# Building the Fourier stage's operands in token parts of 128, behind each transposed attention block

## Chip, cores and metric

One NeuronCore of a Trainium2 chip runs the whole program. The metric is the device time of one execution in microseconds (us), as the median of several runs. The engines of a core have queues of their own, each worked in order: TensorE (PE, with its weight loads as PEld), VectorE (DVE), ScalarE (ACT), GpSimd (POOL), and SyncE (SP) for most DMA.

## What is computed

Three blocks in a row, all in float32: windowed attention (4 batches, 8 heads, 576 tokens, head size 64, window 64), a mixer with a two-dimensional Fourier transform and a hidden layer, and a gated layer. The Fourier part is what the change touches.

```python
X = np.fft.fft(x, axis=1)          # 576 tokens
X = np.fft.fft(X, axis=2)          # 512 channels
mixed = np.real(X).astype(np.float32)
u = x + mixed
un = (u - mu) / np.sqrt(var + 1e-06)
ch = np.maximum(un @ w_ch1, 0.0) @ w_ch2
return (u + ch).astype(np.float32)
```

## The kernel before

**Layout.** The mixer's input and output live in one SBUF tile `uT` of 128 partitions x 4 channel groups x 2304 tokens (channels on partitions, transposed). The channels are permuted so that groups 0 and 1 hold channels 0 to 255 and groups 2 and 3 their mirror images; the real Fourier transform then needs only sums and differences of the two halves.

**Attention** (`attention`, L303 to L408) walks 36 blocks of 64 queries, nine for each batch b. A step computes scores (PE L314), masks and scales them (DVE L317), takes a maximum (DVE L320), exponentials (ACT L322), and one step later transposes (PE L329, copied out by ACT L331 as `pts`) and multiplies with the values (PE L342). `norm` divides (DVE L357, L358, L361). For each full pair of blocks `xt` (L365) transposes the result into one PSUM tile `xt`, of which there is one buffer, and ACT copies it into `uT` (L373). There are five such pieces i for a batch: four of 128 tokens and one of 64. When the last one is issued, `self.xdone = b` (L375).

**Fourier stage** (`dft`, L439 to L522), one call for each batch. L448 and L449 form the sum E and the difference O of the two channel halves over all 576 tokens (1152 elements a partition); L452 and L464 fold tokens t and 576-t onto each other (576 elements). All four run on DVE (`FP` is empty). Each result is split into a rounded high part (ACT, `eh` L457 and `oh` L465) and a remainder (POOL, `el` L458 and `ol` L466). One channel, the middle row, is handled apart: `gr` (POOL L460, L461) from O's first partition, its high part (ACT L462) and remainder (POOL L463) in two rows of `grow`. First-stage products on PE are groups of seven (with `grow`, L482, first and `mm3`, L124 to L126, behind it) or six matmuls; each group is copied out by ACT into `cp` (L491), split by ACT (L492) and POOL (L493). `cp` lies in columns of the E or O tile that are no longer needed: three places for each. The second stage (L496 to L521) makes the spectra and adds them to `uT`.

**Order.** `drive` (L1060 ff.) issues attention and, beside it, two lanes: decoding of weights (L155 to L165) and `dft(0)`, `ln(0)`, `dft(1)`. `dft(2)` and `dft(3)` are issued behind attention with high priority, in the lane `rest`. The tile framework then orders each engine's queue by priority and by a simulated time line, so that instructions can come earlier than they were issued. Behind attention follow the hidden layer (`h`, `acc`, L124 to L126, with `rl` from DVE L670) and the gated layer.

Of the kernel before, what the change touches and what calls it, by code (L numbers as in the profile page):

```python
# [9 lines left out]
F32 = mybir.dt.float32  # L10
F32R = mybir.dt.float32r
I32 = mybir.dt.int32
AF = mybir.ActivationFunctionType
ALU = mybir.AluOpType
# [3 lines left out]
B, H, S, D = 4, 8, 576, 64  # L18
# [23 lines left out]
FP = ()  # L42
# [65 lines left out]
class Kernel:  # L108
# [194 lines left out]
    def attention(self):  # L303
        nc, p, ps = self.nc, self.ap_, self.aps_
# [60 lines left out]
        def xt(n):  # L365
            b, j = divmod(n, NB)
            m, x = 64 if j == NB - 1 else 128, st.pop(("x", n))
            i = j // 2
            t = ps.tile([128, 4, 128], F32, tag="pt", bufs=2, name="xt") if XPT else ps.tile([128, 4, 128], F32, tag="xt", name="xt")
            for c in range(4):  # L370
                nc.tensor.transpose(t[:, c, 0:m], x[:m, 128 * c:128 * c + 128], self.ident[:m, :m])
            t0 = S * b + 128 * i
            nc.scalar.activation(out=self.uT[:, :, t0:t0 + m], in_=t[:, :, 0:m], func=AF.Copy)  # L373
            if j == NB - 1:
                self.xdone = b  # L375

# [34 lines left out]
    def open_dft(self):  # L411
        nc = self.nc
        self.dp, self.dft_es = self.pool("dft", side="left")
        p = self.dp
        self.xdone = -1
        w = [516, 516, 512, 512, 258, 870, 870, 870, 870]
        names = ["cdh", "cdl", "sdh", "sdl", "gt", "csh", "csl", "ssh", "ssl"]
        o = 0
        self.tab = p.tile([128, sum(w)], F32R, name="tab")
        for n, m in zip(names, w):  # L420
            setattr(self, n, self.tab[:, o:o + m])
            o += m
        self.cdh, self.cdl, self.sdh, self.sdl = (t.rearrange("p (k n) -> p k n", k=2) for t in (self.cdh, self.cdl, self.sdh, self.sdl))
        self.csh, self.csl, self.ssh, self.ssl = (t.rearrange("p (k n) -> p k n", k=3) for t in (self.csh, self.csl, self.ssh, self.ssl))
        self.grow = p.tile([128, 290], F32R, name="grow")
        nc.gpsimd.memset(self.grow[:].bitcast(F32), 0.0)
        self.tails = [[p.tile([128, 258], F32R, name=f"tail{i}{x}") for x in "ab"] for i in range(1)]
        for t in self.tails:
            for u in t:
                nc.gpsimd.memset(u[:].bitcast(F32), 0.0)  # L430

    def load_tables(self, i, after):
# [3 lines left out]
        self.nc.gpsimd.tensor_copy(self.tab[:, c.start:c.start + 4], after[:, 0:4])  # L436
        self.tc.keep_in_program_order(self.nc.gpsimd.dma_start(self.tab[:, c], self.aps["tab"][:, c]))

    def dft(self, b):  # L439
        nc, p = self.nc, self.dp  # L440
        x = self.uT[:, :, S * b:S * b + S]
        V, G, A = nc.vector, nc.gpsimd, nc.scalar
        EF = G if b in FP else V
        row = p.tile([1, S], F32, tag="row", name="row")
        nc.sync.dma_start(row, x[0:1, 2])
        E = p.tile([128, 2, S], F32, tag="E", name="E")
        O = p.tile([128, 2, S], F32, tag="O", name="O")
        EF.tensor_tensor(out=E, in0=x[:, 0:2], in1=x[:, 2:4], op=ALU.add)  # L448
        EF.tensor_tensor(out=O, in0=x[:, 0:2], in1=x[:, 2:4], op=ALU.subtract)  # L449
        fold = lambda t: t[:, :, 1:289]  # L450
        rev = lambda t: t[:, :, 575:287:-1]
        EF.tensor_tensor(out=fold(E), in0=fold(E), in1=rev(E), op=ALU.add)  # L452
        eh = p.tile([128, 2, 290], F32R, tag="eh", name="eh")
        el = p.tile([128, 2, 290], F32R, tag="el", name="el")
        oh = p.tile([128, 2, 290], F32R, tag="oh", name="oh")
        ol = p.tile([128, 2, 290], F32R, tag="ol", name="ol")
        A.activation(out=eh[:, :, 0:289], in_=E[:, :, 0:289], func=AF.Copy)  # L457
        G.tensor_tensor(out=el[:, :, 0:289], in0=E[:, :, 0:289], in1=eh[:, :, 0:289], op=ALU.subtract)  # L458
        gr = p.tile([1, 290], F32, tag="gr", name="gr")
        G.tensor_copy(gr[:, 0:1], O[0:1, 0, 0:1])  # L460
        G.tensor_tensor(out=gr[:, 1:289], in0=O[0:1, 0, 1:289], in1=O[0:1, 0, 575:287:-1], op=ALU.add)  # L461
        A.activation(out=self.grow[0:1, 0:289], in_=gr[:, 0:289], func=AF.Copy)  # L462
        G.tensor_tensor(out=self.grow[32:33, 0:289], in0=gr[:, 0:289], in1=self.grow[0:1, 0:289], op=ALU.subtract)  # L463
        EF.tensor_tensor(out=fold(O), in0=fold(O), in1=rev(O), op=ALU.subtract)  # L464
        A.activation(out=oh[:, :, 0:289], in_=O[:, :, 0:289], func=AF.Copy)  # L465
        G.tensor_tensor(out=ol[:, :, 0:289], in0=O[:, :, 0:289], in1=oh[:, :, 0:289], op=ALU.subtract)  # L466
        yield 5000
        ah = p.tile([128, 2, 258], F32R, tag="ah", name="ah")
        al = p.tile([128, 2, 258], F32R, tag="al", name="al")
        bh = p.tile([128, 2, 258], F32R, tag="bh", name="bh")  # L470
        bl = p.tile([128, 2, 258], F32R, tag="bl", name="bl")
        at, bt = self.tails[0]
        ts = [(0, 128), (128, 256), (256, 289)]
        for which in range(2):
            for i, (t0, t1) in enumerate(ts):
                m = t1 - t0
                ps = self.gtile()
                n = 256 if which else 258
                if which:
                    self.mm3(ps[:m, 0:n], [(oh[:, c, t0:t1], ol[:, c, t0:t1], self.sdh[:, c], self.sdl[:, c]) for c in range(2)])  # L480
                else:
                    nc.tensor.matmul(ps[:m, 0:n], lhsT=self.grow[:, t0:t1], rhs=self.gt, start=True, stop=False)  # L482
                    self.mm3(ps[:m, 0:n], [(eh[:, c, t0:t1], el[:, c, t0:t1], self.cdh[:, c], self.cdl[:, c]) for c in range(2)], first=False)
                if i < 2:
                    hi, lo = (bh, bl) if which else (ah, al)
                    hi, lo = hi[:, i, 0:n], lo[:, i, 0:n]
                else:
                    t = bt if which else at
                    hi, lo = t[0:33, 0:n], t[64:97, 0:n]
                cp = (O if which else E)[:m, i // 2, 288 * (i % 2):288 * (i % 2) + n]  # L490
                A.activation(out=cp, in_=ps[:m, 0:n], func=AF.Copy)  # L491
                A.activation(out=hi, in_=cp, func=AF.Copy)  # L492
                G.tensor_tensor(out=lo, in0=cp, in1=hi, op=ALU.subtract)  # L493
                yield 1700

        def stage2(out, lo_, hi_, tail, ch, cl, sl):  # L496
            self.mm3(out, [(hi_[:, k, sl], lo_[:, k, sl], ch[:, k], cl[:, k]) for k in range(2)], last=False)
            nc.tensor.matmul(out, lhsT=tail[:, sl], rhs=ch[:, 2], start=False, stop=False)
            nc.tensor.matmul(out, lhsT=tail[:, sl], rhs=cl[:, 2], start=False, stop=True)

        for c in range(2):
            sl = slice(128 * c, 128 * c + 128)
            pa = self.gtile()
            stage2(pa[:, 0:290], al, ah, at, self.csh, self.csl, sl)
            yield 2000
            pb = self.gtile()
            stage2(pb[:, 0:290], bl, bh, bt, self.ssh, self.ssl, sl)
            bs = p.tile([128, 290], F32, tag="bs", name="bs")
            A.activation(out=bs[:, 0:289], in_=pb[:, 0:289], func=AF.Copy)
            mi = p.tile([128, 290], F32, tag="mi", name="mi")  # L510
            pl = p.tile([128, 290], F32, tag="pl", name="pl")
            V.tensor_tensor(out=mi[:, 0:289], in0=pa[:, 0:289], in1=bs[:, 0:289], op=ALU.subtract)
            V.tensor_tensor(out=pl[:, 0:289], in0=pa[:, 0:289], in1=bs[:, 0:289], op=ALU.add)
            for k, u, w in ((c, mi, pl), (c + 2, pl, mi)):
                V.tensor_tensor(out=x[:, k, 0:289], in0=x[:, k, 0:289], in1=u[:, 0:289], op=ALU.add)
                G.tensor_tensor(out=x[:, k, 289:576], in0=x[:, k, 289:576], in1=w[:, 287:0:-1], op=ALU.add)
            yield 2000
        pa = self.gtile()
        stage2(pa[0:2, 0:290], al, ah, at, self.csh, self.csl, slice(256, 258))
        V.tensor_tensor(out=x[0:1, 2, 0:289], in0=pa[0:1, 0:289], in1=row[:, 0:289], op=ALU.add)  # L520
        V.tensor_tensor(out=x[0:1, 2, 289:576], in0=pa[0:1, 287:0:-1], in1=row[:, 289:576], op=ALU.add)  # L521
        yield 2000  # L522
# [820 lines left out]
```

## Time and profile before

| | |
|---|---|
| median of 3 runs (lowest, highest) | 779.79 us (777.94, 780.92) |
| the profiled execution's own time | 780.66 us |
| its span in the profile | 778.9 us |
| PE, DVE, ACT, POOL busy in the span | 755.9, 491.1, 340.5, 219.2 us |
| mean granted clock of TensorE | 0.991 of full |
| attention and what runs beside it | from 0 to about 150 us |

The profile is one execution, recorded by the hardware profiler. A table by stretches shows how long each engine was busy in each stretch and which share of full speed TensorE's clock was granted. A table of waits says for each idle time of an engine what it waited for. The time line lists instructions with start and duration, and in brackets the idle time ahead of an instruction and what ended it. The listing by source line gives the shortest, the median and the longest duration of one instruction.

### The profile page before, as it was taken

How to read it: one execution, taken by the hardware profiler on the slowest of the kernel's cores; microseconds unless marked ns; L12 is line 12 of the kernel's file. 1: busy time of each engine (PE TensorE's matmuls, PEld its weight loads, DVE VectorE, ACT ScalarE, POOL GpSimd, SP SyncE). 2: the span in 40 equal slices, each digit the busy share in tenths (PEclk: the TensorE clock that was granted, in tenths of full speed). 3: DMA queues.
4: the chain of work that ended last, by engine and by line, in shares of the span. 5: the costliest groups of instructions: out<-in, count | busy, mean ns of one | idle time of the engine just before them, and what ended most of it. 6: DMA issues, size and time to landing. Idle time of an engine off the chain costs nothing.

```text
span 778.9 us, 13646 instructions
## 1 busy us (share of the span) xinstructions
PE 755.9 (97%) x5018; PEld 727.3 (93%) x5018; DVE 491.1 (63%) x1126; ACT 340.5 (44%) x807; POOL 219.2 (28%) x268
## 2 busy tenths in 40 slices
PE   8879899999999999999999999999999999999998
PEld 7779688889999999999999999999999898989898
DVE  5677959594346489794588767644700468574662
ACT  5678797764233666341235323322742343130310
POOL 2135535534203551053712111121591021010100
PEclk9989999999999999999999999999999999999999
DMA  9996672353005878567746943953410020204023
GB/s 275 341 257 182 202 213 69 107 164 122 1 1 157 290 237 322 194 243 262 256 180 232 341 171 104 363 230 109 133 56 1 0 70 12 72 21 142 7 75 121
DMA packets 84770, 123.35 MB, mean 158 GB/s; under 512 B 24416, under 2 KB 61664, under 8 KB 84704
## 3 DMA queue, kind: packets, MB, share of 16 engines
q1 hardware_dynamic: 82912, 119.13, 46.0%
q0 software_dynamic: 576, 2.97, 1.2%
q8 instruction: 39, 0.64, 0.3%
q10 hardware_dynamic: 1216, 0.39, 0.2%
q14 instruction: 27, 0.22, 0.1%
HBM read 91.79 MB, written 30.67 MB: 157 GB/s over the span
## 4 chain that ended last, share of the span: by engine, by line
PE 82%; DVE 7%; DMA 6%; issue 2%; ACT 1%; POOL 0%; SPq 0%; DVEq 0%; ACTq 0%; POOLq 0%
PE w L124 7%; PE w L126 7%; PE w L125 7%; PE g L124 6%; PE c L124 6%; PE c L125 6%; PE c L126 6%; PE g L126 6%; PE g L125 6%; PE pv L342 3%; PE sc L314 3%; PE acc L126 2%; PE acc L125 2%; PE h L124 2%; PE acc L124 2%; PE h L126 2%
## 5 line engine op out<-in xcount | busy, mean ns | idle before, releaser
L164 ACT ACTIVATE set<-dec_w 128x256 fp32r<-128x256 f32 x103 | 41.7, 413 | 62.5 <-PE w L125 27.3
L798 POOL TENSOR_TENSOR u<-u 128x384 f32<-128x384 f32 x15 | 17.7, 1178 | 157.7 <-ACT u L797 139.0
L572 POOL TENSOR_TENSOR rq<-rq,mhalf 128x1 f32<-128x1 f32 (+1 forms) x24 | 15.7, 656 | 163.8 <-DVE rq L571 161.4
L322 ACT ACTIVATE s<-s,mx 128x128 f32<-128x128 f32 x144 | 46.2, 391 | 15.5 <-DVE mx L320 15.4
L158 ACT ACTIVATE dec_g<-dec_s 128x256 f32<-128x256 f32 x88 | 37.5, 429 | 32.9 <-DMA dec_s<-in_wi 16.7
L126 PE MATMUL acc<-rh,set 128*128 128x384 f32 x144 | 48.7, 338 | 0.0
L125 PE MATMUL acc<-rl,set 128*128 128x384 f32 x144 | 48.4, 336 | 0.0
L124 PE MATMUL acc<-rh,set 128*128 128x384 f32 x144 | 47.6, 337 | 0.5 <-DVE uT L655 0.5
L1004 DVE BATCH_NORM_STATS2 st<-u 128x6 f32<-128x512 f32 x18 | 12.4, 692 | 48.6 <-ACT u L1000 48.6
L160 DVE SCALAR_TENSOR_TENSOR dec_w<-dec_g,dec_w 128x256 int32<-128x256 int32 x88 | 41.3, 475 | 2.7 <-ACT dec_g L158 2.2
L314 PE MATMUL sc<-k,q 128*128 128x128 f32 x288 | 40.5, 290 | 2.5 <-DMA k<-in_k 1.4
L798 DVE TENSOR_TENSOR u<-w,u 128x384 f32<-128x384 f32 x44 | 24.3, 552 | 29.4 <-POOL u L798 24.3
L165 DVE TENSOR_TENSOR set<-dec_w,set 128x256 fp32r<-128x256 f32 x83 | 36.8, 451 | 8.2 <-PE h L125 3.8
L314 PEld LDWEIGHTS sc<-k,q 128*128 128x128 f32 x288 | 37.1, 203 | 4.0 <-DVE s L317 1.8
L317 DVE SCALAR_TENSOR_TENSOR s<-sc,mask 128x512 f32<-128x512 f32 x36 | 24.6, 686 | 25.4 <-PE pt L329 14.5
L159 DVE TENSOR_SCALAR dec_w<-dec_s 128x256 int32<-128x256 int32 x88 | 32.3, 377 | 6.4 <-DMA dec_s<-in_wi 3.9
L845 DVE TENSOR_TENSOR uT<-g,uT 128x384 f32<-128x384 f32 x36 | 19.3, 554 | 24.8 <-PE g L126 24.6
L670 DVE SCALAR_TENSOR_TENSOR rl<-h,rh 128x384 fp32r<-128x384 f32 x36 | 19.7, 548 | 20.1 <-ACT rh L669 20.1
L342 PEld LDWEIGHTS pv<-v,pts 128*64 128x64 f32 x576 | 24.7, 147 | 8.0 <-issue 4.5
L342 PE MATMUL pv<-v,pts 128*64 128x65 f32 x576 | 30.0, 237 | 1.6 <-DMA v<-in_v 1.6
L797 ACT ACTIVATE u<-w 128x384 f32<-128x384 f32 x29 | 14.1, 485 | 36.4 <-PE w L126 35.1
L655 DVE TENSOR_TENSOR uT<-acc,uT 128x384 f32<-128x384 f32 x48 | 25.2, 549 | 5.9 <-PE acc L126 5.7
(357 smaller groups left out, 2639.9 us busy)
## 6 DMA issues: line engine op xcount, KB each, us to landing
dec_s<-in_w SPq DMA_DIRECT2D x64, 256.0 KB, 3.3
v<-in_v SPq DMA_DIRECT2D x16, 520.0 KB, 5.4
xht<-xb SPq DMA_DIRECT2D x10, 768.0 KB, 10.0
xhm<-xb SPq DMA_DIRECT2D x10, 768.0 KB, 8.2
xlm<-xb SPq DMA_DIRECT2D x8, 768.0 KB, 9.2
k<-in_k SPq DMA_DIRECT2D x11, 512.0 KB, 5.7
xf<-u SPq DMA_DIRECT2D x18, 256.0 KB, 3.2
p<-xf SPq DMA_DIRECT2D x24, 192.0 KB, 3.6
```

The source lines that it names most:

```text
L124: mm(out, lhsT=lh, rhs=rh, start=first and i == 0, stop=False)
L125: mm(out, lhsT=lh, rhs=rl, start=False, stop=False)
L126: mm(out, lhsT=ll, rhs=rh, start=False, stop=last and i == n - 1)
L158: nc.scalar.activation(out=g, in_=s[:, :, 1].bitcast(F32), func=AF.Prelu, scale=2.0 ** -112, alpha=-2.0 ** 32)
L159: nc.vector.tensor_scalar(out=w, in0=s[:, :, 0], scalar1=29, scalar2=None, op0=ALU.logical_shift_right)
L160: nc.vector.scalar_tensor_tensor(out=w, in0=g[:].bitcast(I32), scalar=3, in1=w, op0=ALU.logical_shift_left, op1=ALU.bitwise_or)
L164: self.nc.scalar.activation(out=hi, in_=f, func=AF.Copy)
L165: (self.nc.gpsimd if self.bp is None else self.nc.vector).tensor_tensor(out=lo, in0=f, in1=hi, op=ALU.subtract)
L314: nc.tensor.matmul(sc[:, hp], lhsT=q[:, hp].rearrange("p a b -> p (a b)"), rhs=k[:, hp, o:o + 128], start=True, stop=True)
L322: nc.scalar.activation(out=s[:, hp], in_=s[:, hp], func=AF.Exp, bias=mx[:, hp:hp + 1])
L342: nc.tensor.matmul(o[r:r + 64, i // 4, 65 * (i % 4):65 * (i % 4) + 65], lhsT=pts[:, i // 2, 64 * (i % 2):64 * (i % 2) + 64], rhs=v[:, 65 * ...
L798: add = lambda eng, o, i, j: eng.tensor_tensor(out=o, in0=i, in1=j, op=ALU.add)
```

## The change

For batches 0 to 2, sums, differences and folds are no longer made in `dft` but piece by piece behind each `uT` copy of attention (`self.folds(b, i, t)`). `fold` adds and subtracts the piece: the lower channel half is read from the PSUM tile `t`, the upper half from `uT`. From piece 2 on, the tokens of that piece are mirrors of earlier ones, and the folds over those columns follow: 96, 128 and 64 columns. The folded difference goes into a tile F of its own, so that O stays whole. `gr` is folded in the same parts. Where the first stage of the batch before has been issued by then, the split into high and low parts is made in two parts as well (columns 65 to 288 behind piece 3, columns 0 to 64 behind piece 4); otherwise it is made whole in `dft`. Batch 3 makes all of it in `dft`, as one part, from `uT`. The product with `grow` moves from the first to the last place of its group. `cp` becomes a tile of its own with two buffers.

```diff
@@ xt
             nc.scalar.activation(out=self.uT[:, :, t0:t0 + m], in_=t[:, :, 0:m], func=AF.Copy)
+            self.folds(b, i, t)
@@ new functions
+    def fold(self, b, x, t, t0, m):
+        V, G = self.nc.vector, self.nc.gpsimd
+        if t0 == 0:
+            self.eo[b] = [self.dp.tile([128, 2, S], F32, tag=n, name=n) for n in ("E", "O", "F")]
+            self.gr[b] = self.dp.tile([1, 290], F32, tag="gr", name="gr")
+        E, O, F = self.eo[b]
+        gr = self.gr[b]
+        c = slice(t0, t0 + m)
+        V.tensor_tensor(out=E[:, :, c], in0=t, in1=x, op=ALU.add)
+        V.tensor_tensor(out=O[:, :, c], in0=t, in1=x, op=ALU.subtract)
+        a, z = max(1, S + 1 - t0 - m), min(289, S + 1 - t0)
+        if a < z:
+            r = slice(S - a, S - z, -1)
+            V.tensor_tensor(out=E[:, :, a:z], in0=E[:, :, a:z], in1=E[:, :, r], op=ALU.add)
+            V.tensor_tensor(out=F[:, :, a:z], in0=O[:, :, a:z], in1=O[:, :, r], op=ALU.subtract)
+            G.tensor_tensor(out=gr[:, a:z], in0=O[0:1, 0, a:z], in1=O[0:1, 0, r], op=ALU.add)
+        if t0 + m == S:
+            V.tensor_copy(F[:, :, 0:1], O[:, :, 0:1])
+            G.tensor_copy(gr[:, 0:1], O[0:1, 0, 0:1])
+
+    def fold_split(self, b, a, z):
...
+        A.activation(out=eh, in_=E[:, :, a:z], func=AF.Copy)
+        G.tensor_tensor(out=el, in0=E[:, :, a:z], in1=eh, op=ALU.subtract)
+        A.activation(out=oh, in_=F[:, :, a:z], func=AF.Copy)
+        G.tensor_tensor(out=ol, in0=F[:, :, a:z], in1=oh, op=ALU.subtract)
+        if a == 0:
...
+
+    def folds(self, b, i, t):
+        if b == B - 1:
+            return
+        t0, m = 128 * i, 64 if i == 4 else 128
+        self.fold(b, self.uT[:, 2:4, S * b + t0:S * b + t0 + m], t[:, 0:2, 0:m], t0, m)
+        if i == 3 and self.dft_read == b - 1:
+            self.fold_split(b, 65, 289)
+        elif i == 4 and b in self.fp:
+            self.fold_split(b, 0, 65)
@@ dft
-        EF.tensor_tensor(out=E, in0=x[:, 0:2], in1=x[:, 2:4], op=ALU.add)
-        EF.tensor_tensor(out=O, in0=x[:, 0:2], in1=x[:, 2:4], op=ALU.subtract)
...
+        if b == B - 1:
+            self.fold(b, x[:, 2:4], x[:, 0:2], 0, S)
+        if b not in self.fp:
+            self.fold_split(b, 0, 289)
+        eh, el, oh, ol = self.fp[b]
...
-                    nc.tensor.matmul(ps[:m, 0:n], lhsT=self.grow[:, t0:t1], rhs=self.gt, start=True, stop=False)
-                    self.mm3(ps[:m, 0:n], [...], first=False)
+                    self.mm3(ps[:m, 0:n], [...], last=False)
+                    nc.tensor.matmul(ps[:m, 0:n], lhsT=self.grow[:, t0:t1], rhs=self.gt, start=False, stop=True)
...
-                cp = (O if which else E)[:m, i // 2, 288 * (i % 2):288 * (i % 2) + n]
+                cp = p.tile([128, 258], F32, tag="cp", bufs=2, name="cp")[:m, 0:n]
...
+        self.dft_read = b
```

## Rows read from the trace of the kernel before

**Rows 1.** Page, span in 40 equal slices: PE busy tenths, granted clock in tenths.
```profile
PE   8879899999999999999999999999999999999998
PEclk9989999999999999999999999999999999999999
```

**Rows 2.** Stretches of 10 us: busy of PE, PEld, DVE, ACT, POOL; clock, DMA, GB/s.
```profile
40.00:50.00 10.00, 6.22 (x76) 5.55 (x74) 9.31 (x17) 7.81 (x24) 2.80 (x5) 0.95 1.10 289
50.00:60.00 10.00, 9.54 (x79) 8.94 (x79) 5.22 (x12) 6.61 (x21) 4.67 (x7) 0.71 0.76 218
...
80.00:90.00 10.00, 8.26 (x88) 6.99 (x86) 10.00 (x19) 7.50 (x18) 5.78 (x7) 1.00 0.73 216
90.00:100.00 10.00, 8.06 (x64) 6.08 (x64) 8.31 (x23) 7.37 (x22) 4.85 (x7) 0.83 0.49 133
...
110.00:120.00 10.00, 10.00 (x91) 9.33 (x90) 6.23 (x10) 8.49 (x26) 5.14 (x8) 1.00 0.82 289
...
130.00:140.00 10.00, 8.73 (x95) 6.94 (x92) 7.50 (x21) 7.84 (x20) 2.64 (x5) 1.00 0.11 29
...
150.00:160.00 10.00, 8.60 (x55) 8.21 (x53) 9.84 (x13) 5.67 (x16) 6.96 (x7) 1.00 0.82 255
160.00:170.00 10.00, 9.31 (x56) 9.00 (x55) 10.00 (x27) 6.80 (x20) 2.98 (x3) 1.00 0.37 112
```

**Rows 3.** PE's waits from 10 to 170 us: total, times, longest, in us.
```profile
PE g L482 <- POOL grow L463: 4.2, 1, 4.2
PE h L124 <- DVE rl L670: 2.1, 2, 1.4
PE pt L329 <- ACT pts L331: 2.0, 3, 1.2
...
PE pt L329 <- ACT s L322: 1.2, 1, 1.2
PE sc L314 <- DVE s L317: 1.1, 1, 1.1
```

**Rows 4.** Time line around batch 0's Fourier operands: start, duration, instruction, idle before.
```profile
42.17 0.38 ACT L373 ACTIVATE uT<-xt 128x256 f32<-128x256 f32 x1
...
43.29 1.35 DVE L448 TENSOR_TENSOR E<-uT 128x1152 f32<-128x1152 f32 x1
...
45.83 0.67 DVE L320 TENSOR_REDUCE mx<-s 128x4 f32<-128x512 f32 x1
...
50.46 0.58 PE L482 MATMUL g<-tab,grow 128*128 128x258 f32 x1 [4.24 <-POOL grow L463]
```

**Rows 5.** Time line of DVE around batch 1's Fourier operands.
```profile
88.79 0.74 DVE L464 TENSOR_TENSOR O<-O 128x576 f32<-128x576 f32 x1
89.46 0.67 DVE L320 TENSOR_REDUCE mx<-s 128x4 f32<-128x512 f32 x1
```

**Rows 6.** Single lines: count, shortest, median, longest ns, first and last start.
```profile
L448 DVE TENSOR_TENSOR E<-uT x4: 1347/1354/1776, 43.3 to 149.8; 128x1152 f32<-128x1152 f32 x4
...
L464 DVE TENSOR_TENSOR O<-O x4: 743/744/1383, 48.2 to 162.5; 128x576 f32<-128x576 f32 x4
...
L512 DVE TENSOR_TENSOR mi<-g,bs x8: 443/450/461, 73.7 to 212.6; 128x289 f32<-128x289 f32 x8
...
L461 POOL TENSOR_TENSOR gr<-O x4: 785/794/995, 46.1 to 159.6; 1x288 f32<-1x288 f32 x4
...
L373 ACT ACTIVATE uT<-xt x20: 366/588/608, 21.0 to 149.4; 128x512 f32<-128x512 f32 x16, 128x256 f32<-128x256 f32 x4
```

**Rows 7.** Time line: copy-out of batch 1's third product group, remainder of its first.
```profile
111.66 0.38 ACT L491 ACTIVATE E<-g 33x258 f32<-33x258 f32 x1 [0.42 <-PE g L126]
...
112.01 0.73 POOL L493 TENSOR_TENSOR al<-E,ah 128x258 fp32r<-128x258 f32 x1
```

**Rows 8.** Time line: a transposed block of batch 2 and its copy into uT.
```profile
96.40 0.63 PE L371 MATMUL xt<-ident,x 128*128 128x128 f32 x2
...
97.84 0.57 ACT L373 ACTIVATE uT<-xt 128x512 f32<-128x512 f32 x1
```

More of the change, by code (lines that the diff above doesn't have):

```diff
@@ L414, in open_dft @@
         p = self.dp
-        self.xdone = -1
+        self.xdone, self.dft_read = -1, -1
+        self.eo, self.fp, self.gr = {}, {}, {}
         w = [516, 516, 512, 512, 258, 870, 870, 870, 870]
@@ L437, in load_tables @@
         self.tc.keep_in_program_order(self.nc.gpsimd.dma_start(self.tab[:, c], self.aps["tab"][:, c]))
+    def fold(self, b, x, t, t0, m):
[18 more added lines that the diff above has]
+    def fold_split(self, b, a, z):
+        G, A = self.nc.gpsimd, self.nc.scalar
+        E, _, F = self.eo[b]
+        if b not in self.fp:
+            self.fp[b] = [self.dp.tile([128, 2, 290], F32R, tag=n, name=n) for n in ("eh", "el", "oh", "ol")]
+        eh, el, oh, ol = (q[:, :, a:z] for q in self.fp[b])
+        A.activation(out=eh, in_=E[:, :, a:z], func=AF.Copy)
[3 more added lines that the diff above has]
+        if a == 0:
+            gr = self.gr[b][:, 0:289]
+            A.activation(out=self.grow[0:1, 0:289], in_=gr, func=AF.Copy)
+            G.tensor_tensor(out=self.grow[32:33, 0:289], in0=gr, in1=self.grow[0:1, 0:289], op=ALU.subtract)
+    def folds(self, b, i, t):
[7 more added lines that the diff above has]
+            self.fold_split(b, 0, 65)
     def dft(self, b):
@@ L442, in dft @@
         V, G, A = nc.vector, nc.gpsimd, nc.scalar
-        EF = G if b in FP else V
         row = p.tile([1, S], F32, tag="row", name="row")
         nc.sync.dma_start(row, x[0:1, 2])
-        E = p.tile([128, 2, S], F32, tag="E", name="E")
-        O = p.tile([128, 2, S], F32, tag="O", name="O")
-        EF.tensor_tensor(out=E, in0=x[:, 0:2], in1=x[:, 2:4], op=ALU.add)
-        EF.tensor_tensor(out=O, in0=x[:, 0:2], in1=x[:, 2:4], op=ALU.subtract)
[L450 to L466, printed above, removed]
+        if b == B - 1:
+            self.fold(b, x[:, 2:4], x[:, 0:2], 0, S)
+        if b not in self.fp:
+            self.fold_split(b, 0, 289)
+        eh, el, oh, ol = self.fp[b]
         yield 5000
@@ L481, in dft @@
                 else:
-                    nc.tensor.matmul(ps[:m, 0:n], lhsT=self.grow[:, t0:t1], rhs=self.gt, start=True, stop=False)
-                    self.mm3(ps[:m, 0:n], [(eh[:, c, t0:t1], el[:, c, t0:t1], self.cdh[:, c], self.cdl[:, c]) for c in range(2)], first=False)
+                    self.mm3(ps[:m, 0:n], [(eh[:, c, t0:t1], el[:, c, t0:t1], self.cdh[:, c], self.cdl[:, c]) for c in range(2)], last=False)
+                    nc.tensor.matmul(ps[:m, 0:n], lhsT=self.grow[:, t0:t1], rhs=self.gt, start=False, stop=True)
                 if i < 2:
```

## Prediction

> **What bounds the kernel now.** I began with the page's slices. A slice is 19.5 us. PE's digits below 9 lie in the first five slices, up to 97 us, and in the very last, and the clock's only one in the third [rows 1]; the long rest has next to nothing for a faster Fourier stage to win. So the question is what PE loses between 40 and 170 us, where this stage's DVE work lies. The table by stretches gives it [rows 2]: PE idle for 3.78 and 0.46 us in 40 to 60, 1.74 and 1.94 in 80 to 100, 1.27 in 130 to 140, 1.40 and 0.69 in 150 to 170. [...] Four places, then: A (40 to 60) 4.2 + 3.1 = 7.3 us, B (80 to 100) 3.7 + 1.4 = 5.1, C (130 to 140) 1.3, D (150 to 170) 2.1; 15.8 us in all.
>
> Next I read PE's waits, to see who ends these idle times [rows 3]. In A it is one wait of 4.2 us for `grow`, the last link of the Fourier operands. In B they are waits for `pts`, the exponentials and the scaled scores, the attention chain itself. In D it is `rl` of the hidden layer. The time line tells why A and B happen [rows 4, 5]: the last copy into `uT` of batch 0 ends at 42.55 (42.17 + 0.38), E begins at 43.29, and the maximum that attention needs runs only at 45.83, behind both E and O; PE starts the first Fourier group at 50.46. In B the maximum of 89.46 stands right behind the fold of O. DVE is busy 9.31 of 10 us in A and 10.00 of 10 in 80 to 90 [rows 2]. In both places DVE's queue, with four long instructions put into it at once, holds up attention.
>
> **The change part by part.** *DVE work.* A fold of 576 elements takes 0.744 us and a sum of 1152 takes 1.354 [rows 6]. That gives 1.06 ns an element and 0.13 us fixed. The only row with one operand in PSUM, `mi` with 289 elements, took 0.45 [rows 6]; the line gives 0.44, so I price the half-PSUM parts by the same line. A part of 256 elements then costs 0.405, of 192 0.34, of 128 0.27, and the copy of F's first column about 0.14. A batch before: 2 x 1.354 + 2 x 0.744 = 4.20 us in 4 instructions. After: eight sums and differences of 256 (3.24), two of 128 (0.54), two folds each of 192, 256 and 128 (2.02), one copy (0.14), 5.94 us in 17 instructions. DVE thus gains 1.74 us of work a batch, 5.2 us for three. As bounds, the longest sum over the median is 1776 / 1354 = 1.31 and the longest fold over the median 1383 / 744 = 1.86 [rows 6]: 5.9 to 11 us a batch; I take the lower, since `mi` varied by 4% only over its eight uses.
>
> [...]
>
> *Where that work lies.* Parts 0 to 2 of a batch run 10 us and more before its end. With DVE busy 6.23 of 10 us PE was still busy for all 10 [rows 2], so there they cost nothing unless such cover is gone, when they cost what they take. At the end of a batch remain part 3 (4 x 0.405 = 1.62) and part 4 (4 x 0.27 + 0.14 = 1.22) in place of 4.20.
>
> *A.* After 42.55 only 1.22 us of DVE work is left; with one attention instruction of 0.67 in between, F and O are ready at about 44.9. Then `gr` (two short POOL instructions, each under the 0.79 of the 288-element one [rows 6]), a ScalarE copy, two short POOL remainders and that of `grow`: some 46.5 to 47.5. PE, which fell idle at 46.22 (50.46 - 4.24), waits 0 to 1.3 us instead of 4.24. That the middle row's product now is last in its group gives this chain another six matmuls of time; it adds no work. Gain 3 to 4.2, taken 3.4. Of the clock's 3.1 I take 2.0: shorter stalls in B too were followed by a clock of 0.83.
>
> *B.* DVE's solid stretch loses 4.2 us, gets 1.22 back and 1.62 just ahead of it: 1.4 to 3.0 us less in a queue on which PE waits. Idle time gains 2.2 (of 3.7), the clock 0.6 (of 1.4). *C.* Here batch 2's four instructions give way to part 4, 3.0 us less on DVE; I take 0.9 of 1.3. *D.* Batch 3 still builds everything at once; nothing.
>
> *Added elsewhere.* The high parts are made in two pieces: by the `uT` copies (512 and 256 elements, 0.588 and 0.37 [rows 6]) each more ScalarE instruction costs 0.15 us, two a batch, beside work. POOL gets four or five short instructions more a batch and was busy 2.6 to 7.0 of 10 us [rows 2]. `cp` has two buffers where it had three places: the third copy-out of a product has to wait for the first remainder. In batch 1 the copy ran at 111.66 and that remainder ended at 112.74 [rows 7], so ScalarE would stand for 1.1 us with attention's `pts` behind it; elsewhere the remainders are ahead. Cost 0 to 1.1, taken 0.3. Each part also waits for ScalarE's `uT` copy, and what is queued behind it on DVE is the next block's scores: 0 to 0.6 us in 15 places, taken 1.2 in all, because PE mostly has other products queued. The DMA of the middle row stays in its place in SP's queue.
>
> **Sum.** A 5.4 + B 2.8 + C 0.9 = 9.1, less 1.5: 7.6 us. The profiled execution took 780.66 (span 778.9 and 1.76 around it), 0.87 above the median of 779.79. 780.66 - 7.6 = 773.1; on the median 772.2.
>
> **Rivals.** *The wait moves.* The framework orders PE's queue by a simulated time line that was wrong by some 4 us in A. If it now places the first Fourier group earlier, PE again stands before its operands. For it: the stall in A is itself such a misplacement. Against it: the real chain behind the last block shrinks by about 3 us whatever the order. Half of A and B is won: 9.1 / 2 - 1.5, about 3 us, 776.8.
>
> *Slower: DVE stands in front of its parts.* Every part reads what ScalarE has just written. In batch 2 a block's transposes ended at 97.03 and the copy began at 97.84 [rows 8]; with its 0.57 DVE could stand 1.4 us with the scores and maximum behind it. Paid in 15 places, that is up to 21 us of DVE; it outweighs the 9.1 from 0.6 us of lost PE time a part. At 0.95 a part it takes 14.3, a net 5 us, with PE's clock falling again: 785. Against it: most of the stage has DVE under 7 tenths.
>
> *All of A, B and C goes.* 7.3 + 5.1 + 1.3 = 13.7: 766.1. For it: their waits trace to the same queue; against it: in B decoding and the layer norm crowd DVE too.
>
> *The early split is not taken* (it needs the first stage of the batch before to be issued). Then the high parts are made whole as now; batch 0 always splits early, so A stands and B and C lose about 0.5 us. This lies inside the forecast.
>
> **How the numbers follow.** Forecast 0.45 (own range 768 to 776.5), the wait moves 0.27 (773 to 780), all goes 0.08, slower 0.20 (779 to 789). 0.5% is about what a measurement of this kernel can tell from no change: below 775.9 is faster, above 783.7 slower. Faster: 0.42 + 0.10 + 0.08 = 0.60. Same: 0.03 + 0.17 + 0.05 = 0.25. Slower: 0.15. The range of 8 in 10 reaches from all that A to C hold (765.8) to the less bad half of the slower case (782.5).
>
> **What would show it.** Right: no wait of PE for `grow` above 1.3 us, clock above 0.85 in the 10 us behind it; parts of about 0.41 us; no maximum of attention behind an instruction of 1.35 us in A and B; D as before. Wrong: DVE idle on the `uT` copy in many places, PE waiting for exponentials behind them, ScalarE waiting for POOL at the third copy-out, or new stalls past 170 us, which no row here announces.

## The result, and the profile after

| | before | changed |
|---|---|---|
| median (lowest to highest, runs) | 780.12 us (777.94 to 781.01, 6) | 771.89 us (771.14 to 774.86, 6) |
| the profiled execution, its span | 780.66, 778.9 us | 772.07, 770.3 us |
| mean granted clock of TensorE | 0.991 | 0.997 |

The ratio is 0.9905, with a 95% interval of 0.9882 to 0.9928: the changed kernel is faster, by 8.2 us on the medians and 7.4 by the ratio. I had forecast 772.2. The time is right; where it came from is partly not what I had worked out.

The page of the changed kernel, busy time by engine and the slices of PE and of the granted clock (compare [rows 1]):

```profile
PE 750.2 (97%) x5018; PEld 723.2 (94%) x5018; DVE 497.8 (65%) x1166; ACT 340.3 (44%) x811; POOL 219.7 (29%) x278
...
PE   8889899899999999999999999999999999999998
...
PEclk9999999999999999999999999999999999999999
```

No slice's clock is below 9 any more. The whole span as a sum of two parts: PE's idle time went from 23.0 us (778.9 - 755.9) to 20.1 (770.3 - 750.2), which is 2.9; what the clock takes, by the estimate (1 - c) x busy with c the mean granted clock, went from 6.8 (0.009 x 755.9) to 2.3 (0.003 x 750.2), which is 4.5. Together 7.4 of the 8.6 us between the two spans. The mean clock is given to 0.001, that is 0.75 us, and the ends of matmuls are modelled; I don't place the remaining 1.2.

By place, the table of stretches of the changed kernel (columns as in [rows 2]):

```profile
0.00:40.00 40.00, 33.65 (x338) 29.88 (x339) 28.22 (x62) 25.80 (x72) 9.38 (x33) 1.00 1.03 309
40.00:50.00 10.00, 7.33 (x81) 6.75 (x80) 9.79 (x22) 8.17 (x27) 6.38 (x10) 0.94 1.11 320
50.00:60.00 10.00, 10.00 (x117) 8.90 (x117) 6.21 (x16) 8.73 (x27) 3.94 (x7) 0.89 0.73 206
...
80.00:90.00 10.00, 8.54 (x85) 7.08 (x85) 10.00 (x27) 8.15 (x24) 4.80 (x8) 1.00 0.77 212
90.00:100.00 10.00, 8.52 (x115) 7.47 (x113) 8.11 (x25) 9.41 (x25) 2.55 (x7) 1.00 0.58 159
...
120.00:140.00 20.00, 18.93 (x188) 16.52 (x189) 16.32 (x38) 13.50 (x31) 7.33 (x12) 1.00 0.14 42
140.00:150.00 10.00, 7.91 (x52) 7.36 (x51) 9.93 (x18) 7.00 (x19) 5.90 (x6) 1.00 0.39 128
150.00:160.00 10.00, 10.00 (x66) 9.81 (x65) 9.46 (x20) 8.05 (x23) 6.18 (x5) 1.00 0.87 260
160.00:170.00 10.00, 10.00 (x63) 9.97 (x62) 9.69 (x24) 3.87 (x9) 1.86 (x3) 1.00 0.28 86
```

Three stretches of the kernel before that [rows 2] lacks, from the same view:

```profile
0.00:40.00 40.00, 34.16 (x330) 30.41 (x331) 24.77 (x51) 24.62 (x69) 8.62 (x30) 0.96 1.04 308
...
120.00:140.00 20.00, 18.48 (x204) 15.82 (x203) 16.82 (x36) 14.35 (x36) 10.33 (x14) 1.00 0.14 42
140.00:150.00 10.00, 9.53 (x107) 8.44 (x105) 4.36 (x12) 9.14 (x19) 4.92 (x9) 1.00 0.22 61
```

| place | before: idle + clock | after: idle + clock | gain | forecast |
|---|---|---|---|---|
| 0 to 40 | 5.84 + 1.37 | 6.35 + 0 | 0.9 | none |
| A, 40 to 60 | 4.24 + 3.08 | 2.67 + 1.54 | 3.1 | 5.4 |
| B, 80 to 100 | 3.68 + 1.37 | 2.94 + 0 | 2.1 | 2.8 |
| C, 120 to 140 | 1.52 + 0 | 1.07 + 0 | 0.4 | 0.9 |
| D, 140 to 170 | 2.56 + 0 | 2.09 + 0 | 0.5 | 0 |

That makes 7.0 us. The first line is not put down to the change: the clock before 40 us is 0.96 or 1.00 in the profiles of the kernels below, and what that stretch loses runs from 5.3 us (e5) to 9.5 (e6), two kernels that treat batch 0 alike. A single span against another is therefore good to a few us only; the medians carry the times.

PE's waits from 10 to 170 us in the changed kernel (total, times, longest; compare [rows 3]):

```profile
PE xt L371 <- ACT oh L471: 2.7, 1, 2.7
PE pt L329 <- ACT pts L331: 2.0, 2, 1.1
PE h L124 <- DVE rl L704: 1.5, 1, 1.5
...
PE xt L371 <- DVE O L452: 0.6, 1, 0.6
```

The wait of 4.2 us for `grow` is gone. In its place stands a wait of 2.7 us of the transposes of attention's next block, and the one for `rl` has become a single one of 1.5. The time line of A shows where the first of these comes from (compare [rows 4]):

```profile
43.55 0.28 DVE L451 TENSOR_TENSOR E<-xt,uT 128x128 f32<-128x128 f32 x1
...
44.97 0.97 POOL L476 TENSOR_TENSOR grow<-gr,grow 1x289 fp32r<-1x289 f32 x1 [0.56 <-ACT grow L475]
45.21 0.88 DVE L456 TENSOR_TENSOR E<-E 128x128 f32<-128x128 f32 x1
...
46.71 0.69 DVE L361 TENSOR_TENSOR x<-pv,rd 128x512 f32<-128x512 f32 x1
...
47.55 0.41 PE L371 MATMUL xt<-ident,x 128*128 128x128 f32 x2 [2.67 <-ACT oh L471]
```

`grow` was ready at 45.94, and no wait for it is left. But the product that makes `x` of the next block began only at 46.71 and ended at 47.40: DVE, busy for 9.79 of the 10 us, had ahead of it two maxima, three decoding instructions, part 4 and a fold of 128 elements that took 0.88 instead of 0.28, beside POOL's `grow`. The profile puts the wait down to the split `oh` (47.25 to 47.54 on ScalarE). I read it as `x`, which these transposes take as operand: in e2 below `x` ran at 46.72, the transposes began at 47.56, and there the profile names `x`, as it does for the same wait in e10 (2.5 us).

The second place is the entry into the hidden layer. Attention's last copy into `uT` ended at 149.8 before and at 137.8 now, 12 us earlier. These are not 12 us of lost time: by the table the stretches up to 140 us gain 6.5, and part of the rest is order, since batch 2's first `oh` group ran at 143.46 before, ahead of attention's last copy, and runs at 140.91 now, behind it. From 137.8 on DVE has batch 3's whole sums in its queue (start, duration, instruction):

```profile
137.87 1.80 DVE L451 TENSOR_TENSOR E<-uT 128x1152 f32<-128x1152 f32 x1 [0.39 <-ACT uT L373]
139.59 1.34 DVE L452 TENSOR_TENSOR O<-uT 128x1152 f32<-128x1152 f32 x1
...
144.24 1.28 DVE L460 COPY F<-O 128x2 f32<-128x2 f32 x1
...
146.11 0.55 DVE L704 SCALAR_TENSOR_TENSOR rl<-h,rh 128x384 fp32r<-128x384 f32 x1
...
146.71 0.44 PE L124 MATMUL h<-xh,set 128*128 128x384 f32 x1 [1.46 <-DVE rl L704]
```

PE reaches its first wait for `rl` only at 145.25, because until then it has two of batch 2's three `oh` groups and transposes of the layer norm to work on. That cover is what the experiments turned out to be about.

### The profile page after: what moved, and what is told of

Its sections match the earlier page's. It is cut to its first block, busy times and chain, and to the rows that moved or that the text cites. A ratio compares the mean times of both kernels' runs of the same rounds, so it can differ in the third digit from the quotient of the medians.

```text
span 770.3 us, 13705 instructions
## 1 busy us (share of the span) xinstructions
PE 750.2 (97%) x5018; PEld 723.2 (94%) x5018; DVE 497.8 (65%) x1166; ACT 340.3 (44%) x811; POOL 219.7 (29%) x278
## 4 chain that ended last, share of the span: by engine, by line
PE 88%; DVE 6%; DMA 2%; ACT 1%; issue 1%; SPq 1%; POOL 0%; ACTq 0%; POOLq 0%
PE w L124 7%; PE w L126 7%; PE w L125 7%; PE g L124 7%; PE g L126 6%; PE g L125 6%; PE c L124 6%; PE c L126 6%; PE c L125 6%; PE acc L126 3%; PE acc L125 3%; PE h L124 3%; PE h L126 3%; PE h L125 3%; PE acc L124 3%; DMA v<-in_v 2%
## 5 line engine op out<-in xcount | busy, mean ns | idle before, releaser
L342 PEld LDWEIGHTS pv<-v,pts 128*64 128x64 f32 x576 | 22.9, 139 | 7.0 <-issue 4.4
L342 PE MATMUL pv<-v,pts 128*64 128x65 f32 x576 | 27.6, 228 | 1.4 <-DMA v<-in_v 1.4
L703 ACT ACTIVATE rh<-h 128x384 fp32r<-128x384 f32 x36 | 17.3, 481 | 25.8 <-PE h L126 25.7
```

The lines of the kernel that those rows point to most:

```text
L342: nc.tensor.matmul(o[r:r + 64, i // 4, 65 * (i % 4):65 * (i % 4) + 65], lhsT=pts[:, i // 2, 64 * (i % 2):64 * (i % 2) + 64], rhs=v[:, 65 * ...
```

## Experiments

Each run is timed against the kernel before on the same chip; that kernel's medians were 780.1 to 780.5 us on all of them, so the medians below are also set side by side. Numbers in brackets are the range and the number of runs.

| run | what it is | median, us | ratio, 95% interval |
|---|---|---|---|
| e1 | before, only `grow`'s product last | 777.37 (774.46 to 781.48, 10) | 0.9961, 0.9935 to 0.9986 |
| e4 | changed, all batches whole | 778.10 (775.57 to 780.03, 10) | 0.9961, 0.9945 to 0.9978 |
| e5 | changed, parts for batch 0 only | 775.29 (774.15 to 778.48, 6) | 0.9939, 0.9913 to 0.9965 |
| e6 | changed, parts for batches 0 and 1 | 773.10 (771.37 to 776.84, 4) | 0.9907, 0.9872 to 0.9942 |
| e2 | changed, `grow`'s product first | 778.56 (777.24 to 779.67, 10) | 0.9971, 0.9954 to 0.9989 |
| e3 | changed, parts from SBUF alone | 777.65 (775.47 to 780.20, 10) | 0.9964, 0.9943 to 0.9985 |
| e7 | changed, batch 3 in parts too | 772.51 (771.41 to 773.63, 4) | 0.9893, 0.9869 to 0.9917 |
| e8 | e2 and e7 together | 773.09 (771.70 to 775.83, 4) | 0.9902, 0.9866 to 0.9939 |
| e9 | e3 and e7 together | 772.07 (771.74 to 773.17, 4) | 0.9889, 0.9863 to 0.9914 |
| e10 | changed, six buffers for `cp` | 773.66 (770.78 to 774.54, 4) | 0.9899, 0.9870 to 0.9928 |

### How much is the product's place, how much the parts

e1 makes in the kernel before only the move of the product:

```diff
-                    nc.tensor.matmul(ps[:m, 0:n], lhsT=self.grow[:, t0:t1], rhs=self.gt, start=True, stop=False)
-                    self.mm3(ps[:m, 0:n], [...], first=False)
+                    self.mm3(ps[:m, 0:n], [...], last=False)
+                    nc.tensor.matmul(ps[:m, 0:n], lhsT=self.grow[:, t0:t1], rhs=self.gt, start=False, stop=True)
```

> The kernel before with one edit: the middle row's product (L482) stands last in its group instead of first. Theory (the gain comes from cutting up DVE's work at the end of a batch): PE's wait of 4.2 us in A was for the last link of a chain that DVE began late; the maximum of attention still stands behind E and O, so at most 1 to 1.5 us of that wait goes, 0 to 2 us faster in all, 778 to 780. Rival (the wait for the middle row was the matter): most of the 4.2 us and of the clock's 3 us goes, 773 to 775.

e4 is the other side: it keeps all of the change but the parts, so that every batch is summed and folded whole in `dft`.

```diff
     def folds(self, b, i, t):
-        if b == B - 1:
+        if 1:
             return
...
-        if b == B - 1:
+        if 1:
             self.fold(b, x[:, 2:4], x[:, 0:2], 0, S)
```

> The changed kernel with the parts undone: every batch makes sums, differences and folds whole in dft, from uT; F and cp keep tiles of their own and the middle row's product stays last. Theory: the gain goes, 778 to 781, and the maximum of attention stands behind sums of 1.35 us again at about 45 and 83 us. Rival (the separate tiles for F and cp, which free E and O earlier, or the product's place carry it): 774 or less.

The two agree within their intervals, 777.4 and 778.1 us; e4 lies in its range, e1 0.6 us below its own, and neither comes near its rival. So the place of the product gives about 2 to 3 us, and F and a `cp` of its own neither add to that nor take from it by more than can be measured. The row of A says why it is no more: the wait has gone from `grow` to the link ahead of it. First e1, then e4, PE's longest wait from 10 to 170 us:

```profile
PE g L124 <- ACT eh L457: 3.2, 1, 3.2
```

```profile
PE g L124 <- ACT eh L469: 3.2, 1, 3.2
```

4.2 us for `grow` became 3.2 us for `eh`. The stretches of A in e1:

```profile
40.00:50.00 10.00, 6.77 (x79) 6.09 (x78) 9.29 (x17) 7.81 (x23) 2.42 (x4) 0.98 1.12 293
50.00:60.00 10.00, 10.00 (x91) 9.19 (x91) 6.92 (x14) 8.06 (x24) 6.33 (x9) 0.85 0.77 226
```

That is 3.2 us idle and 1.6 of clock, 4.9 in all against 7.3 before and 4.2 in the changed kernel: most of what A gained is there without any parts. The parts are then worth the distance from e4 to the changed kernel, 778.1 - 771.9 = 6.2 us. Not all of it can be placed. Of the 6.5 us between the two spans, 2.6 lie behind 40 us (0.7 in A, 1.1 in B, nearly all the rest in 60 to 80 and 100 to 120), 2.5 in the stretch before 40 us, which differs from run to run.

### Which batches

e5 and e6 make the parts for batch 0 alone, and for batches 0 and 1 (the second line in `dft` is changed alike):

```diff
-        if b == B - 1:
+        if b != 0:
             return
```

```diff
-        if b == B - 1:
+        if b not in (0, 1):
             return
```

> The changed kernel with parts for batch 0 only; batches 1 to 3 make everything whole in dft. Theory (each batch's parts relieve DVE's queue at that batch's end): A is won as in the changed kernel, B and C are not; the last copy of attention into uT ends 2 to 5 us before the 149.8 us of the kernel before, and the time is 775 to 779. Rival (the parts of batch 0 carry nearly all): the last copy ends near 138, as in the changed kernel.

> The changed kernel with parts for batches 0 and 1; batches 2 and 3 whole in dft. Theory: the last copy into uT ends between that of the run with batch 0 alone and the 137.8 us of the changed kernel, about 140 to 143; time 773 to 778. Rival (batch 2's parts do nothing, C being small): 137.8 us again.

From whole to batch 0, to batches 0 and 1, to all three: 778.1, 775.3, 773.1, 771.9. Steps of 2.8, 2.2 and 1.2 us; the intervals of neighbours overlap, so only the fall from the first to the last is told. Both times lie in their ranges, the ends of attention do not: its last copy ended at 140.7 us in e5, 9 us before 149.8 and not 2 to 5, and at 142.8 in e6, later than in e5. So the end of attention alone does not tell the kernel's time. With batch 1 whole, place B does not recover. The stretch of e5:

```profile
80.00:100.00 20.00, 16.85 (x143) 14.46 (x144) 16.09 (x35) 14.13 (x35) 9.48 (x11) 0.74 0.61 168
```

3.15 us idle and 0.26 x 16.85 = 4.4 us of clock, against 2.94 and nothing in the changed kernel, while A in e5 had a clock of 1.00 and only 2.6 us idle. With batch 1 in parts B lost 2.6 us in e6 and 2.9 in the changed kernel, with it whole 4.0 in e1 and e4. A and B thus go with their own batch, as the prediction's places had it. C does not: with batch 2 whole it lost 1.2 us in e4, 1.0 in e5 and 2.0 in e6, against 1.1 in the changed kernel.

### Do the product's place and the PSUM operand matter with the parts there

e2 is the changed kernel with the product back in first place, e3 the changed kernel with both operands of the parts from SBUF:

```diff
-        self.fold(b, self.uT[:, 2:4, ...], t[:, 0:2, 0:m], t0, m)
+        self.fold(b, self.uT[:, 2:4, ...], self.uT[:, 0:2, S * b + t0:S * b + t0 + m], t0, m)
```

> The changed kernel with one edit undone: the middle row's product first in its group again. Theory: within 1.5 us of the changed kernel, 771 to 773.5. Rival (the middle row's place is half or more of the gain): 775 or more, with PE waiting 2 us or more for the remainder of grow around 47 us.

> The changed kernel with the lower half of each part read from uT in SBUF instead of from the transposes' PSUM tile. Theory (the queue's length at the end of a batch matters, not where operands lie): within 2 us of the changed kernel, 770 to 774, parts of 256 elements at 0.41 us in the median with some stretched beside POOL; PE's one wait for O behind a transposed block (0.6 us) goes, since the PSUM tile is free earlier. [...]

Either small edit costs about 6 us, nearly all that the parts had brought. Both times miss the theory's range. e2's lies in its rival's, but the rival's sign is absent: PE waited 0.23 us for `grow` around 46 us. In e3 the median of the E parts was 0.42 us, where the theory had 0.41. Read the other way round, the parts bring 6.2 us with the product last and 780.15 - 778.56 = 1.6 with it first, so neither edit has one price. The 6 us aren't lost where the edits stand: attention's last copy into `uT` ends at 137.8 and 138.1, as in the changed kernel (137.8), and by the stretches up to 140 us e2 had lost as much as the changed kernel, 14.6 us, and e3 1.2 less. It is lost right behind. Entry of e2, stretch and time line of DVE and PE:

```profile
140.00:150.00 10.00, 5.74 (x26) 5.42 (x25) 9.69 (x22) 4.65 (x11) 4.18 (x5) 0.85 0.29 90
```

```profile
137.87 1.84 DVE L451 TENSOR_TENSOR E<-uT 128x1152 f32<-128x1152 f32 x1 [0.96 <-ACT uT L373]
139.63 1.89 DVE L452 TENSOR_TENSOR O<-uT 128x1152 f32<-128x1152 f32 x1
...
144.88 1.26 DVE L460 COPY F<-O 128x2 f32<-128x2 f32 x1
...
146.12 0.55 DVE L704 SCALAR_TENSOR_TENSOR rl<-h,rh 128x384 fp32r<-128x384 f32 x1
```

```profile
141.44 0.33 PE L126 MATMUL h<-xh,set 128*128 128x384 f32 x1
141.61 0.85 PE L124 MATMUL acc<-rh,set 128*128 128x384 f32 x4
146.72 0.54 PE L124 MATMUL h<-xh,set 128*128 128x384 f32 x1 [4.26 <-DVE rl L704]
147.06 0.52 PE L125 MATMUL h<-xl,set 128*128 128x384 f32 x1
```

and of e3 the same stretch, and the wait:

```profile
140.00:150.00 10.00, 5.79 (x26) 5.47 (x24) 9.92 (x22) 4.69 (x10) 5.55 (x5) 0.84 0.27 82
```

```profile
PE h L124 <- DVE rl L704: 4.2, 1, 4.2
```

`rl` runs at 146.12, at the very time of the changed kernel (146.11). But PE has nothing else left at 142.5: batch 2's `oh` groups, which bridge 141 to 145 in the changed kernel, come only at 154.15 here (154.33 in e3). DVE's order differs too: the layer norm's short instructions, done by 137.5 in the changed kernel, stand between and behind the sums here, at 141.45 and 146.05. PE stands 4.26 us, and the clock falls behind that: 0.52 a matmul of 384 columns where it was 0.33. In 140 to 150 e2 loses 4.26 + 0.15 x 5.74 = 5.1 us, the changed kernel 2.1; in 150 to 170 it loses 0.9 more, the changed kernel nothing. These 3.9 us are most of the 5.2 between the two spans; in the stretches ahead, gains and losses nearly cancel. e3 loses the same 3.9 us from 140 on, but with 1.2 us less lost ahead that places only half of its 5.4.

One of those gains is A, and it shows the same thing from the other side. PE in e2:

```profile
46.00 0.51 PE L514 MATMUL g<-tab,grow 128*128 128x258 f32 x2 [0.23 <-POOL grow L476]
...
47.56 0.41 PE L371 MATMUL xt<-ident,x 128*128 128x128 f32 x2 [0.32 <-DVE x L361]
```

`x` is as late as in the changed kernel. But with `grow`'s product first PE had a Fourier group ahead of the transposes, from 46.00 on, and A lost 1.39 us at a clock of 1.00 instead of 4.2. So e2 is better in A and worse at the entry: which work stands in PE's queue ahead of a late operand counts.

So the theory became: what decides the 6 us is batch 3's whole burst on DVE at the entry, and the two edits only change what PE has queued there.

### Batch 3 in parts

If so, taking the burst away must restore e2 and e3, and do little for the changed kernel, which had cover. The edit, in `folds` and in `dft`:

```diff
-        if b == B - 1:
+        if 0:
```

> The changed kernel with batch 3 in parts behind its transposed blocks as well. Theory (what attention wins is given back at the entry into the hidden layer, where batch 3's whole sums, decoding and the remainder rl share DVE's queue): PE's wait for rl at about 145 us (1.5 us) goes, DVE has 4 us less at 138 to 146, time 768 to 771. Rival (the wait at the entry is for decoding, which runs there whatever batch 3 does, and the parts now crowd attention's last blocks): 771 to 775.

> As the run before, but with the middle row's product first in its group. With that product first and batch 3 whole, the time was 778.6, attention's last copy ended at 137.8 as in the changed kernel, and PE then waited 4.3 us for rl. Theory (the loss is DVE's burst at the entry, not the product's place): with batch 3 in parts the wait falls below 1.5 us and the time comes within 2 us of the run before, 768 to 773. Rival (the product's place costs PE time of its own): 775 or more.

> The kernel of the run with the lower half of the parts read from SBUF, with batch 3 made in parts as well. Theory (the loss of that run, 777.7 us against 771.9 us of the changed kernel, is the 4.2 us wait of TensorE for `rl` behind batch 3's whole sums at the entry into the hidden layer, with the lower clock after it): 771 to 774.5 us, and the wait of TensorE for `rl` under 2 us. Rival (reading the lower half from SBUF is itself dearer, because the parts then wait for ScalarE's copies): 776 to 779 us, with the waits of VectorE for copies of `uT` over 8 us in all.

Entry of e8, stretch and wait:

```profile
140.00:150.00 10.00, 8.33 (x51) 7.78 (x50) 7.77 (x24) 8.14 (x20) 3.46 (x5) 1.00 0.34 110
```

```profile
PE h L124 <- DVE rl L704: 0.8, 1, 0.8
```

and of e9:

```profile
140.00:150.00 10.00, 8.46 (x52) 7.97 (x51) 9.46 (x29) 8.31 (x22) 3.09 (x4) 1.00 0.53 173
```

```profile
DVE E L451 <- ACT uT L373: 4.7, 6, 1.1
```

e2's 778.6 became 773.1 in e8, e3's 777.7 became 772.1 in e9: 5.5 and 5.6 us from one edit that touches batch 3 alone. The wait for `rl` went from 4.3 and 4.2 to 0.8 and 1.5, and the clock of the stretch to 1.00. With batch 3 in parts it makes no measurable difference whether `grow`'s product is first or last, or whether the lower half comes from PSUM or SBUF. e9's rival, that parts from SBUF stand waiting for ScalarE's copies, is ruled out by the row of `uT`: 4.7 us of DVE's time in six waits, where the changed kernel has 4.9 in six.

But the two kernels come to this in different ways. First `rl` in e8, then `rl` and PE's wait in e9:

```profile
146.84 0.54 DVE L704 SCALAR_TENSOR_TENSOR rl<-h,rh 128x384 fp32r<-128x384 f32 x1
```

```profile
142.25 0.55 DVE L704 SCALAR_TENSOR_TENSOR rl<-h,rh 128x384 fp32r<-128x384 f32 x1
142.84 0.45 PE L124 MATMUL h<-xh,set 128*128 128x384 f32 x1 [1.54 <-DVE rl L704]
```

In e9 the theory holds: with the burst gone `rl` runs 4.1 us earlier than in e3 (1.5 of it because attention ended earlier, at 136.6), and PE, still without cover (its `oh` groups start at 148.74), waits 1.5 us. In e8 `rl` runs no earlier than in e2. The burst is gone, but decoding stands there, with DVE idle for 2.2 us before 144.92; PE only comes to the wait later, because attention ended at 139.7 and an `oh` group is back ahead of it, at 143.51. So what the runs show is that the loss comes and goes with a long stand of PE before `rl`, with nothing else queued. That batch 3's burst is what delays `rl` is shown by e9 against e3, and not by e8 against e2. Each of these edits also changes the order of the queues, and no run holds that order fixed.

e7 is the miss of this group, and lies in its rival's range; the rival's sign is there, since `rl` ran at 145.98 behind decoding, 0.1 us earlier than in the changed kernel. Its wait for `rl` did fall, from 1.5 to 0.8, and 140 to 150 held 9.12 us of PE work instead of 7.91; but its time, 772.5, is that of the changed kernel. Its attention ended at 139.6 instead of 137.8, and 120 to 140 lost 1.7 us instead of 1.07. Parts in batch 3 take from attention what they give to the entry. No kernel here beats the changed one by more than can be measured; e7, e9 and it lie within 0.7 us.

### The two buffers of `cp`

```diff
-                cp = p.tile([128, 258], F32, tag="cp", bufs=2, name="cp")[:m, 0:n]
+                cp = p.tile([128, 258], F32, tag="cp", bufs=6, name="cp")[:m, 0:n]
```

> The changed kernel with six buffers for the tiles `cp` in place of two. Theory (the two buffers cost next to nothing, as the prediction put it, 0.3 us): within 1 us of the changed kernel, 771 to 773 us. Rival (the waits that the two buffers add hold ScalarE or VectorE back and cost more than that): 768 to 770.5 us.

The one wait of ScalarE for a remainder, 1.0 us in the changed kernel, is gone, and the time is no shorter: 773.7 with runs from 770.8 to 774.5. That is 0.7 us above the 773 that the theory allowed, and the range holds the changed kernel's time; a gain from more buffers is not to be seen.

## Why the prediction was right, and where it was not

**What bounds the kernel.** Right. Of the 8.6 us between the spans 6.1 lie in the places named and 0.9 before 40 us. Total idle time and clock are the two parts, and PE's wait for `grow` went, as said. The clock's 3.1 us in A and 1.4 in B, of which the sum takes 2.0 and 0.6, are shown by no run as lost time, and are an estimate of mine, (1 - c) x busy from [rows 2]; what the runs show is the granted clock itself, 0.95 and 0.71 in A and 0.83 in 90 to 100 before, 0.94, 0.89 and 1.00 in the changed kernel.

**DVE work.** Right for the parts, too low for folds and copies. Twelve parts of 256 took 0.41 where I had 0.405, three of 128 took 0.27 to 0.28 where I had 0.27. By single line in the changed kernel (count, shortest, median, longest in ns):

```profile
L451 DVE TENSOR_TENSOR E<-xt,uT x15: 269/415/425, 21.7 to 112.0; 128x256 f32<-128x256 f32 x12, 128x128 f32<-128x128 f32 x3
...
L457 DVE TENSOR_TENSOR F<-O x10: 274/478/961, 32.8 to 143.6; 128x192 f32<-128x192 f32 x3, 128x256 f32<-128x256 f32 x3, 128x128 f32<-128x128 f32 x3, 128x576 f32<-128x576 f32 x1
...
L460 DVE COPY F<-O x4: 153/164/1284, 23.0 to 144.2; 128x2 f32<-128x2 f32 x4
```

DVE's busy time rose by 497.8 - 491.1 = 6.7 us where I had 5.2 for three batches. By line, the twenty folds took 9.99 us in all where my prices give 7.6 (before, eight took 6.76 where they give 5.95), and the four copies 1.76 where they give 0.56. That parts 0 to 2 cost nothing is shown for batch 1 alone: they run from 51.2 to 66.5, and PE was busy for all of 50 to 80. Batch 2's run from 91.6 to 100.7, inside B, where PE lost 1.5 us in 90 to 100, and batch 0's before 40 us, where idle time rose by 0.5.

**A.** The wait for `grow` went, but the size was not right, 3.1 us instead of 5.4, and the source only in part: e1 brings A from 7.3 to 4.9 us by the product's place alone, which I had folded into this gain without a price of its own. The failed step is "PE, which fell idle at 46.22, waits 0 to 1.3 us instead of 4.24". I followed the chain to `grow` with one attention instruction between the last copy and the parts. Between the last part of O at 43.75 and `x` at 46.71 the queue had a maximum, two decoding instructions, both folds and two short instructions of attention, and what was late next was not `grow` but that `x`. Of the clock's 3.1 us 1.5 came back, and I had 2.0; the wait of 2.67 was followed by a clock of 0.89 in the next 10 us. The size was there to be had: A lost 2.55 us in e5 and 1.39 in e2, both at a clock of 1.00, with the queues in another order.

**B and C.** B gave 2.1 for 2.8, but 1.4 of it from the clock (I had 0.6) and 0.7 from idle time (I had 2.2). C gave 0.4 for 0.9, and e4 to e6 do not tie it to batch 2's parts.

**D.** "Batch 3 still builds everything at once; nothing" came out at 0.5 and was yet the weakest sentence. It took the entry as it stood, while the whole of attention moved 12 us forward against the weights' decoding and batch 3's burst. e2 and e3 show what could have happened: 6 us given back, 3.9 of them placed here. Neither the sum nor a rival had that; the forecast's time rests here on cover that I had not looked for.

**Added costs.** I took 1.5 us. The wait for `cp` did not come in batch 1; one of 1.05 us came at 189 us, and e10 finds no cost in it. Waits of DVE for the copy into `uT` there were, 4.9 us in six places and 2.2 in a seventh, some 0.5 us a part; PE's own waits show 0.6 us of that, for the one buffer of `xt` that O held. I had 1.2.

**Rivals.** "The wait moves" was half true in A: it moved, but to attention's queue on DVE rather than to a group placed too early, and at 2.7 us rather than 4.2. "DVE stands in front of its parts" exists at half of its price and falls on DVE, not on PE; e9, where both operands of each part come from that copy, has no more of it. "All of A, B and C goes" did not come in any run; 4.2, 2.9 and 1.1 us of loss stayed in the three places. The early split was taken in batches 0 and 1 and not in batch 2, whose `eh` was made whole at 113.86 us.

**Why the sum still fitted.** A, B and C gave 3.5 us less than forecast. Against that stand the 1.5 us of added costs, which the stretches already hold, 0.5 in D, 0.9 before 40 us and 0.2 of idle time behind 170 us, and the 1.2 us that I can't place. Some of this is luck: the 0.9 us before 40 us are 1.4 of clock less 0.5 of idle time, in a stretch that differs from run to run. (The low end of the range of 8 in 10 should read 766.1 and not 765.8, by the same 13.7 us from 779.79.)

## What to carry to other kernels

Cutting a burst on a side engine into pieces is worth what the main engine waits for behind that burst, but ask what stands next in the same queue: here the wait moved from the Fourier operands to the next attention block and lost a third of its size, not all, and part of that third came from the product's place. When a stage ends earlier, look at the entry of the stage behind it: an untouched burst there can take back most of the gain, and whether it does depends on what happens to be queued as cover, so that two edits which cost nothing by themselves each seemed to cost 6 us. Before an unexplained loss is put down to the edit that showed it, compare the time at which the edited stage ended, what each stretch lost and what stood in each queue there.

## What the runs showed of the hardware

**A copy of two elements took 1.28 us.** The copy of F's first column took 0.15 to 0.17 us, and 1.28 at 144.24 in the changed kernel, while POOL made batch 3's remainder of 578 elements from 143.57 to 145.49; in e2 it took 1.26. In the changed kernel the copy ended at 145.52, 0.03 us behind POOL's instruction. I had priced it at 0.14. The fold at 143.57 ran wholly beside the same remainder and took 0.74, the median of the folds before [rows 6]; why the copy took so long is not shown.

**With one operand in PSUM no part was stretched.** e7 and e9 differ only in where the lower half comes from. Their E parts:

```profile
L451 DVE TENSOR_TENSOR E<-xt,uT x20: 269/412/426, 22.6 to 139.8; 128x256 f32<-128x256 f32 x16, 128x128 f32<-128x128 f32 x4
```

```profile
L451 DVE TENSOR_TENSOR E<-uT x20: 269/418/862, 23.9 to 137.6; 128x256 f32<-128x256 f32 x16, 128x128 f32<-128x128 f32 x4
```

The longest is 0.426 with PSUM and 0.862 without (at 115.55, with the part of O at 116.33 at 0.86 too), at nearly the same median. In the changed kernel the part of O at 108.58, with one operand in PSUM, ran wholly beside POOL's `al` (108.56 to 109.20) and took 0.41. Of the folds there, with both operands in SBUF, one of 256 elements took 0.96 at 109.84 (0.41 at 41.02), beside POOL's `tail0a` (109.67 to 110.52), and one of 128 took 0.27 at 89.12, wholly beside POOL's `set` (88.76 to 89.98). Folds were thus stretched beside POOL in some places and not in others; what decides it is not shown. In time the place of the lower half was worth nothing here, 772.5 us in e7 against 772.1 in e9.

**The clock.** A stall of 1.46 us of PE at 145.25 in the changed kernel left the granted clock at 1.00 in its stretch of 10 us, one of 2.67 there at 44.88 was followed by 0.94 and 0.89 in its stretch and the next, one of 4.26 at 142.46 in e2 by 0.85, with matmuls of 384 columns at 0.52 instead of 0.33 us behind it. In B stalls of 2.9 us in all went with a clock of 1.00 in the changed kernel and of 0.91 in e2, so here the sum of the idle time in a stretch does not tell it.
